# First unit's inverse from diagonal blocks of 16 with one more merge level, its norms from squares by feature, and a new order of steps

## The chip, the cores and the metric

The kernel runs on one core of a Trainium2 chip. The metric is the device time of one execution in microseconds. A profile of one execution gives each instruction's engine, start and length: PE is the matrix engine (PEld its weight loads), DVE the vector engine, ACT the scalar engine, POOL the GpSimd engine, SP the queue that issues the DMAs.

## What is computed

Two layers. The first is a delta-rule recurrence over 768 tokens for 4 batches and 8 heads of width 48; the second is a mixture of four causal attention experts, of which two per token are kept.

```python
k_n = k / (norm(k) + 1e-6)
for t in range(S):                          # state: 48 x 48 per batch and head
    y[t] = q[t] @ state
    state = state + beta[t] * outer(k_n[t], v[t] - k_n[t] @ state)
x = y, heads side by side                   # 768 x 384 per batch
logits = x @ w_gate                         # the two largest of four are kept; softmax over them
for e in range(4):
    a = softmax(causal(q_e k_e^T / 8))      # q_e, k_e, v_e = x @ wq[e], wk[e], wv[e], width 64
    out += weight(e) * (a @ v_e) @ wo[e]
```

## The kernel before

The recurrence is done in blocks of 64 tokens. Within a block the 64 updates follow from the inverse of a unit triangular 64 x 64 matrix, made of the Gram matrix of the block's keys, beta and the norms; from block to block only the state is carried. The work is cut into 6 units (half of the batches, a third of the tokens: units 0 to 2 and 3 to 5 are two sequences of three), and each unit has 4 chunks (index c) of one 64-token block for 16 heads.

For unit n the steps are, by their names in the order list:

- lg, lq, lc: loads of keys, queries and the keys with values. `gr` (L211): Gram matrices on PE, copied to the tile tt. `gq` (L229): K times Q, masked by DVE.
- `si` (L238): DVE transposes the 32 x 32 blocks of tt into B, so that one partition holds one matrix of 32 x 32. `pre` 0 to 5 (L258): the norms by three Newton steps from the sums of squares ss, the factors aa (beta over norm squared), and B times -aa.
- `sv` (L308): the inverse, 30 rank-one steps of a multiply (L305) and an add (L303), then two finishing instructions. For units 1 to 5 it runs on POOL. For unit 0 rows 0 to 8 run on DVE, each instruction cut in two halves, and rows 9 to 31 on POOL (`sg`, L325).
- `so`, `sn` (L338, L334): DVE transposes the inverse back to tt and, untransposed, to TN. `m10` to `m15` (merge1, L343) and `m2n.c` (merge2, L353): matmuls that join the two 32-blocks of each 64-block.
- `ks`, `u`, `q`, `s`, `y` per chunk: the chain proper. u needs the merged inverse, s makes the next state. `hx` spreads the result by DMA.
- `pj`, `pv`: projections; `mx`, `mp`, `mr`, `sc`, `av`, `nm`, `ft`, `fo`: attention and output; `gt`: gates.

The first unit's norms come from a separate load of its keys by token (kt): `sq` (L250) squares on POOL, `sr` (L255) sums on DVE. For units 1 to 5 ss is the diagonal of the Gram matrix.

All instructions of all engines are issued in the order of the list `ORDER` (L35), written out by hand or by a planner: each engine runs its own instructions in that order and waits by semaphores for the others. An entry `+N` is N fillers: matmuls of zeros into a corner of the tile po that nobody reads. The list has 382 of them, one more is issued at the top; 297 stand ahead of u0.0. PSUM tiles named pm_ have three buffers, so a group of matmuls waits until the copies of an earlier group are done. B and tt have two buffers each: unit n + 2 can begin its `gr` when unit n's chain is done with tt. Profile lines with L109 are matmuls, whatever step they belong to.

Of the kernel before, what the change touches and what calls it, by code (L numbers as in the profile page):

```python
# [40 lines left out]
+109 gq0.0 so0 +33 gq0.3 +11 m10.0 w0 sn0 m10.1 +3 m20.0 lg2.0 w5 si1 pre1.0 pre1.1 m20.3 u0.0 pre1.2 pre1.3 w2 m20.2  # L41
s0.0 w1 lc0.2 vt0.2 m20.1 ks0.1 y0.0 pre1.4 gq0.2 u0.1 +3 q0.1 s0.1 vs lq1.3 lq1.2 pre1.5 sv1.1 lc0.3 gq1.0 ks0.2 y0.1
gr2.0 +4 gq1.1 hx0.1.0 sv1.2 q0.2 u0.2 +5 s0.2 lq2.0 gq1.2 vt0.3 sv1.3 +1 ks0.3 gq1.3 y0.2 +1 pj0.0.2 q0.3 lg2.1 u0.3
pj0.0.0 lg2.3 sv1.4 sv1.5 s0.3 sv1.6 y0.3 gr2.3 lg2.2 sv1.7 +6 pv0.0.1 sv1.8 gq2.0 pv0.0.0 sv1.9 sv1.10 sv1.11 sv1.12
sv1.13 mx0.0.0.1 sv1.14 sv1.15 lc1.0 vt1.0 sv1.16 mx0.1.0.0 mx0.0.0.0 lq2.1 w6 mx0.1.0.1 sv1.17 sv1.18 +1 gq2.1 sv1.19
# [745 lines left out]
```

## Time and profile before

| | |
|---|---|
| times of 3 runs | 523.9 us median, 519.34 to 529.47 |
| the profiled execution | 521.83 us, span 520.0 us |
| busy | PE 465.0, PEld 408.9, DVE 320.4, ACT 261.1, POOL 245.9 us |
| fillers | 383, 51.9 us of PE's busy time |
| inputs and outputs | HBM read 24.74 MB, written 4.72 MB |

A row of a timeline is start, length, engine, line, operation, written tile <- read tiles, shapes, count; a bracket at the end is the idle time of the engine before it and what ended it ("issue": nothing that the profile shows). A row of a table of stretches is the stretch, its length, and each engine's busy time in it with the count of instructions. A matmul of fp32 data shows as two passes.

### The profile page before, as it was taken

The page shows a single profiled execution, that of the slowest core. Times are in us where ns is not written, and L with a number is a line of the kernel's source. Part 1 is how long each engine was busy: PE and PEld are TensorE (multiplying, and loading weights), DVE is VectorE, ACT ScalarE, POOL GpSimd, SP SyncE. Part 2 cuts the span into 40 slices and gives each one's busy share as a digit, 9 for nine tenths or more (in the row PEclk, how much of TensorE's full clock was granted, in tenths as well). Part 3 has the DMA queues.
Part 4 walks back from the last instruction along what each step waited for, and adds up shares of the span by engine and source line. Part 5 has one row for each costly group of instructions (what it writes and reads, how often), then busy time and mean ns, then how long its engine had stood idle before and what let it go on. Part 6 is the DMA issues. An engine that isn't in the chain of part 4 may idle for free.

```text
span 520.0 us, 23164 instructions
## 1 busy us (share of the span) xinstructions
PE 465.0 (89%) x10271; PEld 408.9 (79%) x10271; DVE 320.4 (62%) x745; ACT 261.1 (50%) x642; POOL 245.9 (47%) x422
## 2 busy tenths in 40 slices
...
DMA packets 19396, 33.31 MB, mean 64 GB/s; under 512 B 2912, under 2 KB 9440, under 8 KB 19296
## 3 DMA queue, kind: packets, MB, share of 16 engines
...
q14 instruction: 19, 0.16, 0.1%
HBM read 24.74 MB, written 4.72 MB: 57 GB/s over the span
## 4 chain that ended last, share of the span: by engine, by line
PE 68%; DVE 15%; ACT 9%; issue 6%; DMA 1%; SPq 0%; ACTq 0%; DVEq 0%
PE po L109 13%; PE xu L109 7%; PE py L109 6%; DVE tm L305 2%; DVE B L303 2%; ACT QA L486 2%; ACT QA L483 1%; DVE mx L564 1%; ACT KH L489 1%; ACT KA L483 1%; DVE QL L494 1%; DVE KA L492 1%; DVE B L243 1%; DVE B L240 1%; ACT VS L510 1%
## 5 line engine op out<-in xcount | busy, mean ns | idle before, releaser
L303 POOL TENSOR_TENSOR B<-B,tm 128x30 f32<-128x30 f32 (+9 forms) x150 | 78.6, 524 | 11.7
L305 POOL TENSOR_TENSOR tm<-B 128x30 f32<-128x30 f32 (+9 forms) x150 | 74.3, 495 | 10.9
L109 PE MATMUL po<-VS,at 128*64 128x65 f32 x1344 | 51.8, 230 | 6.6 <-ACT rs L634 4.5
L109 PEld LDWEIGHTS po<-VS,at 128*64 128x64 f32 x1344 | 45.0, 142 | 13.0 <-ACT rs L634 5.9
L109 PE MATMUL po<-zb 128*128 128x252 bf16 x383 | 51.9, 287 | 2.5 <-ACT rs L634 1.3
L141 POOL TENSOR_TENSOR kv<-kv,nt 128x384 f32<-128x384 f32 x24 | 19.9, 830 | 60.9 <-DMA kv<-in_kv_dram 48.6
L109 PEld LDWEIGHTS <-zb 128*128 128x128 bf16 x383 | 37.7, 103 | 8.8 <-DVE zb L114 1.1
L372 POOL MEMSET tt<- 32x1024 f32 x10 | 9.5, 946 | 49.6 <-PE pm__2366 L109 13.0
L633 ACT ACTIVATE os<-po 128x128 f32<-128x128 f32 x48 | 13.3, 278 | 35.1 <-PE po L109 35.0
L109 PE MATMUL py<-qf,sb 48*48 48x64 f32 x704 | 24.5, 218 | 2.3 <-issue 1.9
L446 ACT ACTIVATE xh<-py 112x384 fp32r<-112x384 f32 x24 | 11.8, 492 | 28.4 <-PE py L109 28.4
L448 DVE TENSOR_TENSOR xh<-py,xh 112x384 fp32r<-112x384 f32 x24 | 13.4, 557 | 20.4 <-ACT h L447 20.4
L109 PEld LDWEIGHTS <-identb 128*128 128x128 bf16 x192 | 19.2, 100 | 8.2 <-issue 2.0
L294 POOL TENSOR_TENSOR B<-B,nn 128x1024 f32<-128x1024 f32 x5 | 11.9, 2371 | 28.5 <-DVE nn L293 28.4
L109 PEld LDWEIGHTS py<-qf,sb 48*48 48x48 f32 x704 | 21.3, 120 | 5.0 <-issue 2.4
L427 DVE TENSOR_TENSOR sb<-sb,xu 112x384 f32<-112x384 f32 x20 | 11.1, 553 | 22.2 <-PE xu L109 22.1
L109 PE MATMUL py<-pm,ub 64*48 64x64 f32 x768 | 18.0, 228 | 5.2 <-issue 5.0
L409 DVE TENSOR_TENSOR xs<-kv,xu 128x384 f32<-128x384 f32 x22 | 12.1, 552 | 14.8 <-PE xu L109 8.1
L243 DVE STREAM_TRANSPOSE B<-tt 32x1024 f32<-32x1024 f32 x10 | 19.9, 1994 | 0.2
L109 PE MATMUL xu<-sb,kf 48*64 48x48 f32 x704 | 16.8, 229 | 3.6 <-issue 3.2
L109 PEld LDWEIGHTS py<-pm,ub 64*48 64x48 f32 x768 | 14.6, 129 | 6.1 <-issue 5.6
L109 PE MATMUL xu<-xs,tt 64*64 64x48 f32 x768 | 18.5, 227 | 0.8 <-issue 0.7
...
## 6 DMA issues: line engine op xcount, KB each, us to landing
...
kf<-in_kq_dram SPq DMA_DIRECT2D x24, 256.0 KB, 4.1
qf<-in_kq_dram SPq DMA_DIRECT2D x24, 256.0 KB, 3.5
...
wst<-in_wqk_dram SPq DMA_DIRECT2D x3, 256.0 KB, 4.8
wst<-in_wvg_dram SPq DMA_DIRECT2D x1, 256.0 KB, 6.2
```

Of the source, the lines that this page charges most:

```text
L109: T.matmul(o, lhsT=a, rhs=b, start=start, stop=stop, skip_group_check=True)
L141: G.tensor_tensor(vt, vt, PR[n]["nt"][:, c * NP:c * NP + NP, None].to_broadcast([128, NP, HD]), op=OP.mult)
L243: V.transpose(B[r:r + 32], gf[r:r + 32, :, 0:32].rearrange("p t j -> p j t"))
L294: G.tensor_tensor(B, B, bc(nn, 32), op=OP.mult)
L303: e.tensor_tensor(X[:, a:b, i + 1:], X[:, a:b, i + 1:], tv, op=OP.add)
L305: e.tensor_tensor(tv, R[:, :, i + 1:].to_broadcast([128, w, m]), X[:, a:b, i:i + 1].to_broadcast([128, w, m]), op=OP.mult)
L409: V.tensor_tensor(eight(XB), eight(vt), PX, op=OP.subtract)
L427: V.tensor_tensor(eight(new), eight(state(n, c)), SP, op=OP.add)
L446: S.activation(hi, Y[:, :, 0:3], AF.Copy)
L448: V.tensor_tensor(lo, Y[:, :, 0:3], hi, op=OP.subtract)
L483: S.activation((KA if isk else qa)[h, es, :, t], P[h], AF.Copy)
L633: S.activation(os[:, :, e], O[:, :, 0:EH], AF.Copy)
```

## The change

Unit 0 no longer inverts 32 x 32 matrices. The Gram mask keeps only the two diagonal 16 x 16 blocks of each, 14 steps on DVE invert both at once (28 instructions of 2 x i x (15 - i) elements a partition), and nothing of it runs on POOL. The off-diagonal block goes, negated, from the Gram's PSUM to a new tile GO by one more ACT copy per half chunk. After so0 and sn0 a new level `m00.c.0`, `m00.c.1` (merge0) joins the 16-blocks: 32 matmuls and an ACT copy, then 64 matmuls and two DVE adds, into tt and TN. merge1 of unit 0 is cut in four parts instead of two.

The norms of unit 0 come from the keys by feature that are loaded anyway: ACT squares the tile (into the other tt buffer), 16 matmuls a chunk with a column of ones sum over the features into the tile xu, and one DVE copy moves the 32 sums to ss. The kt input is gone. Unit 1's keys are now loaded at the top, ahead of the first kv and q. The memsets of QL and KH stand at the top, with ten for the new tiles.

`ORDER` is new throughout. It has 384 fillers, of which 254 stand ahead of u0.0; si1 and the first norm steps of unit 1 stand between sn0 and the new level. Units 1 to 5 have the same steps as before.

```diff
--- before.py
+++ after.py
...
+NL = 1
...
 ORDER = """
-fr3 +41 gr0.3 sq0 sr0 sq1 sr1 sq2 +8 gr0.0 sq3 sr2 sr3 lq1.1 pre0.0 +4 gr0.1 lg1.3 pre0.1 pre0.2 pre0.3 lg1.1 kc3 fr1
-kc1 fr0 +6 gr0.2 pre0.4 vt0.0 cb si0 pre0.5 kc0 sv0.1 sv0.2 sv0.3 sv0.4 sv0.5 sv0.6 sv0.7 fr2 sg10 sv0.8 sv0.9 sg11
-lc0.1 sv0.10 sv0.11 sg12 w3 sv0.12 sv0.13 sv0.14 sv0.15 lg1.0 +31 gr1.1 sg13 sg14 sg15 vt0.1 sv0.16 lq1.0 sv0.17
-sv0.18 lg1.2 sv0.19 ks0.0 sv0.20 sv0.21 +33 gr1.2 sv0.22 sv0.23 sv0.24 sv0.25 +4 gr1.3 sv0.26 sg16 sg17 sg18 sg19 sg20
-sg21 sg22 kc2 sg23 sv0.27 +4 gr1.0 sg24 sg25 sg26 sg27 sg28 +10 gq0.1 sv0.28 sv0.29 sv0.30 sg29 sg30 sv0.32 sg32 w4
...
++39 gr0.2 sq3 sq0 sq2 +12 gr0.1 +5 sr0 lc0.1 sq1 sr2 gr1.2 +3 sr1 +6 gq0.1 sr3 pre0.0 pre0.1 +1 gr1.0 pre0.2 w0 pre0.3
+pre0.4 +4 gr1.1 +5 gr0.3 +13 gr0.0 si0 pre0.5 sv0.1 +7 gr1.3 sv0.2 +4 gq0.3 sv0.3 sv0.4 sv0.5 sv0.6 sv0.7 sv0.8 sv0.9
+sv0.10 sv0.11 sv0.12 sv0.13 +19 gq0.0 lq1.0 +57 gq1.0 sv0.14 sv0.16 so0 w4 sn0 si1 pre1.0 lq1.1 pre1.1 +32 m00.0.0
+m00.1.0 w3 vt0.0 +31 m00.0.1 cb pre1.2 pre1.3 +9 m10.0 kc2 +7 m20.0 pre1.4 m00.1.1 ks0.0 u0.0 +5 s0.0 pre1.5 sv1.1 w2
+sv1.2 vt0.1 m10.1 m00.3.0 kc3 kc1 m20.1 sv1.3 kc0 m00.2.0 ks0.1 +9 m00.2.1 sv1.4 sv1.5 m00.3.1 m10.2 m10.3 y0.0 u0.1
+sv1.6 sv1.7 sv1.8 lg2.1 sv1.9 sv1.10 gq0.2 sv1.11 lc0.2 sv1.12 sv1.13 sv1.14 q0.1 vs1 s0.1 vt0.2 +6 ks0.2 y0.1 m20.2
...
-    KT = [KF[:, 384 * c:384 * c + 384] for c in range(CH)]
+    cst = cp.tile([128, 240], F32, name="cst")
+    bta = cp.tile([128, NU, 32], F32, name="bta")
+    csb = wk.tile([128, 264], F32, name="csb", tag="at", bufs=5)
+    load_k(0, 0)
+    nc.sync.dma_start(cst, consts[:, 0:240])
+    for c in range(1, CH):
+        load_k(0, c)
+    nc.sync.dma_start(bta, beta)
     for c in range(CH):
-        load_k(0, c)
-    cst = cp.tile([128, 240], F32, name="cst")
-    for c in range(CH):
-        nc.sync.dma_start(KT[c], kt[c])
-        if c == 1:
-            nc.sync.dma_start(cst, consts[:, 0:240])
-    bta = cp.tile([128, NU, 32], F32, name="bta")
-    nc.sync.dma_start(bta, beta)
+        load_k(1, c)
     load_chain(0, 0)
-    csb = wk.tile([128, 264], F32, name="csb", tag="at", bufs=5)
     nc.sync.dma_start(csb, consts[:, 240:504])
     for c in range(CH):
         load_q(0, c)
+    on = cp.tile([128, 1], F32, name="on")
+    V.memset(on, 1.0)
...
-    def free_rows(r, e):
-        G.memset(QL[64 - r:128 - r, e].bitcast(F32), 0.0)
-        G.memset(KH[64 - r:128 - r, e].bitcast(F32), 0.0)
+    slot = lambda k, h: KF[:, 260 * k + 256 * h:260 * k + 256 * h + 256].rearrange("p (t i) -> p t i", t=NP)
+    GO = [[slot(k, h) for k in ks for h in range(2)] for ks in ((0, 8), (4, 10))]
+    AS = [slot(2, h) for h in range(2)]
+    for c in range(CH):
+        G.memset(GO[0][c], 0.0)
+    for t in AS + GO[1]:
+        G.memset(t, 0.0)
+    for r, x in HA:
+        G.memset(QL[64 - r:128 - r, x::2].bitcast(F32), 0.0)
+        G.memset(KH[64 - r:128 - r, x::2].bitcast(F32), 0.0)
...
-    NSV = 1
-    PS = 9
-    BP = KF[:, 0:(32 - PS) * 32].rearrange("p (a b) -> p a b", b=32)
-    SQ = [KF[:, 1536 + 384 * c:1920 + 384 * c] for c in range(CH)]
-    WS = [KF[:, 1536:2592].rearrange("p (a b) -> p a b", b=32)] + LB
+    SQ = [TG[1][:, NP * c:NP * c + NP] for c in range(CH)]
...
         for p, i, _, r, t, _ in by(1):
-            if n:
+            if n >= NL:
                 mm(g[i // 4][t:t + 64, i % 4], x[r:r + HD, p], x[r:r + HD, p], True)
                 continue
             for h in range(2):
...
                 V.tensor_tensor(o[:, :, 32:], g[f][:, :, 32:], kmask[:, None, :].to_broadcast([128, 4, 32]), op=OP.mult)
                 S.activation(o[:, :, 0:32], g[f][:, :, 0:32], AF.Copy)
+            if n < NL:
+                S.activation(GO[n][c][:, 4 * f:4 * f + 4, 0:16], g[f][:, :, 32:48], AF.Copy, scale=-1.0)
...
         if c == 0:
             solve_vars(0)
-        G.tensor_tensor(SQ[c], KT[c], KT[c], op=OP.mult)
+        S.activation(SQ[c], LD[0, c], AF.Square)
     def square_sum(c):
-        V.tensor_reduce(PR[0]["ss"][:, NP * c:NP * c + NP], SQ[c].rearrange("p (a b) -> p a b", b=HD), axis=AX.X, op=OP.add)
+        for p, i, _, r, t, _ in by(1):
+            mm(XS[t:t + 64, i // 4, 4 * c + i % 4:4 * c + i % 4 + 1], SQ[c][r:r + HD, p], on[r:r + HD], True)
+        if c == CH - 1:
+            V.tensor_copy(PR[0]["ss"].rearrange("p (c f i) -> p f c i", c=CH, f=2), XS[:, :, 0:16].rearrange("p f (c i) -> p f c i", c=CH))
...
-            B = pr["B"]
-            bc = lambda t, w: t[:, None, :].to_broadcast([128, w, 32])
-            if n < NSV:
-                for a, b in ((PS, 32), (0, PS)):
-                    V.scalar_tensor_tensor(B[:, a:b], B[:, a:b], -1.0, bc(aa, b - a), op0=OP.mult, op1=OP.mult)
-                S.activation(BP, B[:, PS:], AF.Copy)
+            e = G if n else V
+            if n < NL:
+                Z = blocks(n)
+                V.tensor_scalar(nn, aa, -1.0, None, op0=OP.mult)
+                e.tensor_tensor(Z, Z, by_col(nn), op=OP.mult)
             else:
                 V.tensor_scalar(nn, aa, -1.0, None, op0=OP.mult)
-                G.tensor_tensor(B, B, bc(nn, 32), op=OP.mult)
...
+                G.tensor_tensor(pr["B"], pr["B"], nn[:, None, :].to_broadcast([128, 32, 32]), op=OP.mult)
+    def blocks(n):
+        z = LB[n % 2].rearrange("p a b -> p (a b)").rearrange("p (s x) -> p s x", s=2)[:, :, 16:528]
+        return z.rearrange("p s (a c) -> p s a c", c=32)[:, :, :, 16:32]
+    by_col = lambda t: t.rearrange("p (s i) -> p s i", s=2)[:, :, None, :].to_broadcast([128, 2, 16, 16])
+    by_row = lambda t: t.rearrange("p (s j) -> p s j", s=2)[:, :, :, None].to_broadcast([128, 2, 16, 16])
     def solve_step(n, i):
         B, aa = PR[n]["B"], PR[n]["aa"]
-        tmp = TM
-        e = V if n < NSV else G
-        r = PS if n < NSV else 32
-        if i <= 30:
-            w = min(i, r)
-            h = w // 2 if n < NSV else 0
-            rank1(e, B, B[:, i:i + 1], tmp, i, [x for x in ((0, h), (h, w)) if x[0] < x[1]])
-        elif i == 31:
+        e, size = G if n else V, 16 if n < NL else 32
+        Z = blocks(n) if n < NL else B[:, None]
+        k = 2 if n < NL else 1
+        if i < size - 1:
+            m = size - 1 - i
+            tv = TM[:, 0:k * i * m].rearrange("p (s a b) -> p s a b", s=k, a=i)
+            bc = lambda x: x.to_broadcast([128, k, i, m])
+            if k == 1:
+                Z, tv = B, tv[:, 0]
+                bc = lambda x: x.to_broadcast([128, i, m])
+                e.tensor_tensor(tv, bc(Z[:, i:i + 1, i + 1:]), bc(Z[:, 0:i, i:i + 1]), op=OP.mult)
+                e.tensor_tensor(Z[:, 0:i, i + 1:], Z[:, 0:i, i + 1:], tv, op=OP.add)
+            else:
+                e.tensor_tensor(tv, bc(Z[:, :, i:i + 1, i + 1:]), bc(Z[:, :, 0:i, i:i + 1]), op=OP.mult)
+                e.tensor_tensor(Z[:, :, 0:i, i + 1:], Z[:, :, 0:i, i + 1:], tv, op=OP.add)
+        elif i == size - 1:
             if n:
                 G.affine_select(B, B, pattern=[[-1, 32], [1, 32]], compare_op=OP.is_gt, fill=0.0, base=0,
                                 channel_multiplier=0)
+            if 0 < n < NL:
+                G.memset(B[:, 0:16, 16:32], 0.0)
         else:
-            e.tensor_tensor(B[:, 0:r], B[:, 0:r], aa[:, 0:r, None].to_broadcast([128, r, 32]), op=OP.mult)
-            e.tensor_copy(B.rearrange("p j i -> p (j i)")[:, 0:33 * r - 32:33], aa[:, 0:r])
...
+            if n < NL:
+                e.tensor_tensor(Z, Z, by_row(aa), op=OP.mult)
+            else:
+                e.tensor_tensor(B, B, aa[:, :, None].to_broadcast([128, 32, 32]), op=OP.mult)
+            e.tensor_copy(B.rearrange("p j i -> p (j i)")[:, 0:1024:33], aa)
     def st_nat(n):
         pr = PR[n]
...
     def st_out(n):
         V.transpose(TG[n % 2][:, :, 32:].rearrange("p t i -> p i t"), PR[n]["B"].rearrange("p l i -> p i l"))
-    lanes = lambda n: WS[0] if n == 0 else LB[n % 2]
+    def merge0(n, c, k):
+        tt, a, GR = TG[n % 2], AS[c % 2], range(0, 128, 32)
+        W = ps.tile([128, 2, NP, 16], F32, name="pm_", bufs=3)
+        for i in range(NP):
+            t = NP * c + i
+            for g in GR:
+                if k == 0:
+                    mm(W[g:g + 32, 0, i], GO[n][c][g:g + 32, i], tt[g:g + 32, t, 48:64], True)
+                else:
+                    mm(W[g:g + 32, 0, i], TN[g:g + 32, t], a[g:g + 32, i, 16:32], True)
+                    mm(W[g:g + 32, 1, i], a[g:g + 32, i], TN[g:g + 32, t, 0:16], True)
+        if k == 0:
+            S.activation(a[:, :, 16:32], W[:, 0], AF.Copy)
+        else:
+            for j, o in enumerate((tt[:, NP * c:NP * c + NP, 48:64], TN[:, NP * c:NP * c + NP, 0:16])):
+                V.tensor_tensor(o, o, W[:, j], op=OP.add)
+    lanes = lambda n: LB[n % 2]
     def merge1(n, k):
-        gf = TG[n % 2]
-        W = ps.tile([128, 16, 32], F32, name="pm_", bufs=3)
-        for i in range(16):
-            t = 16 * k + i
+        gf, m = TG[n % 2], NP if n < NL else 16
+        W = ps.tile([128, m, 32], F32, name="pm_", bufs=3)
+        for i in range(m):
+            t = m * k + i
             for r, _ in HA:
                 mm(W[r:r + 32, i], gf[r + 32:r + 64, t, 0:32], gf[r + 32:r + 64, t, 32:64], True)
         for r, _ in HA:
-            S.activation(lanes(n)[r:r + 32, 1 + 16 * k:17 + 16 * k], W[r:r + 32], AF.Copy, scale=-1.0)
+            S.activation(lanes(n)[r:r + 32, 1 + m * k:1 + m * k + m], W[r:r + 32], AF.Copy, scale=-1.0)
...
-    step("vs", ones)
-    for i in (*range(PS + 1, 31), 32):
-        step("sg", solve_pool, i)
+    for k in range(3):
+        step("vs", ones, k)
...
+                step("m0", merge0, n, k, j)
...
-    c[:, 208:240] = (i % 32)[:, None] >= np.arange(32)[None, :]
+    c[:, 208:240] = ((i % 32)[:, None] >= np.arange(32)) & ((i % 32 // 16)[:, None] == np.arange(32) // 16)
...
```

More of the change, by code (lines that the diff above doesn't have):

```diff
@@ L41 @@
[L41 to L45, printed above, removed]
@@ new lines @@
++5 u0.2 m20.3 lq1.2 sv1.15 sv1.16 sv1.17 sv1.18 sv1.19 sv1.20 lc0.3 vt0.3 w1 w5 hx0.1.0 q0.2 sv1.21 gq1.1 s0.2 vs0
+sv1.22 +2 pv0.0.0 lq1.3 gr2.1 ks0.3 lc1.0 vt1.0 sv1.23 y0.2 w6 lg2.2 pj0.0.2 sv1.24 sv1.25 gq1.3 q0.3 lq2.1 u0.3 +11
+y0.3 s0.3 pv0.0.1 gr2.2 sv1.26 sv1.27 sv1.28 +4 gq1.2 ks1.0 +1 gq2.1 sv1.29 sv1.30 hx0.3.0 lg3.0 sv1.31 sv1.32 so1
+lg2.3 pj0.0.0 sn1 pj0.1.0 pj0.1.2 q1.0 lq2.0 m11.0 +11 m11.1 cl1 m21.0 mx0.1.1.3 pv0.1.0 mx0.0.1.3 lg2.0 mx0.0.1.2
+lq2.2 u1.0 mx0.0.0.0 vs2 mx0.0.0.1 mx0.1.1.2 mp0.0 mx0.1.0.1 lc1.1 mx0.1.0.0 s1.0 mr0.0 mp0.1 pv0.1.1 m21.1 vt1.1 gt0
@@ new lines @@
+ks1.1 gr2.3 y1.0 sc0.0.0.0 lc1.3 vt1.3 mr0.1 +1 gr2.0 si2 u1.1 q1.1 lq2.3 sc0.0.3.0 lg3.1 sc0.0.2.0 pre2.0 sc0.0.1.0
+av0.0.0 m21.3 av0.0.3 s1.1 sc0.1.2.0 av0.0.1 m21.2 av0.0.2 lc1.2 pre2.1 pre2.2 vt1.2 gq2.2 ks1.2 y1.1 sc0.1.1.0
+sc0.1.0.0 sc0.1.3.0 u1.2 nm0.0 lg3.2 pre2.3 q1.2 pre2.4 gr3.2 pre2.5 ft0.0 av0.1.3 hx1.1.0 s1.2 sv2.1 gq2.3 sv2.2
+sv2.3 sv2.4 sv2.5 +3 ks1.3 lg3.3 sv2.6 y1.2 gq2.0 sv2.7 lq3.0 pj1.0.2 sv2.8 sv2.9 pj1.0.0 q1.3 u1.3 lq3.1 fo0.0.0
+mx1.0.0.1 sv2.10 sv2.11 av0.1.0 sv2.12 sv2.13 s1.3 sv2.14 sv2.15 sv2.16 lc2.0 y1.3 gr3.3 sv2.17 mx1.1.0.0 sv2.18 +1
@@ L96, with tile_kernel @@
+mx5.1.0.0 sc5.0.3.2 mx5.1.0.6 mp5.1 sc5.0.3.0 ft4.1 pv5.1.1 mr5.1 av5.0.3 sc5.1.0.0 sc5.1.0.1 sc5.1.0.2 sc5.1.1.2
+sc5.1.1.0 av5.1.0 sc5.1.1.1 sc5.1.2.2 sc5.1.2.1 av5.1.1 sc5.1.2.0 fo4.1.1 sc5.1.3.0 gt5 sc5.1.3.1 nm5.0 av5.1.2
+sc5.1.3.2 fo4.1.0 ft5.0 av5.1.3 fo5.0.1 fo5.0.0 nm5.1 ft5.1 +13 fo5.1.1 fo5.1.0
 """
 @with_exitstack
-def tile_kernel(ctx, tc, kq, kv, kt, beta, wqk, wvg, wo, consts, out):
+def tile_kernel(ctx, tc, kq, kv, beta, wqk, wvg, wo, consts, out):
     nc = tc.nc
@@ L240, in st_in @@
         V.transpose(B, gf[:, :, 32:].rearrange("p t j -> p j t"))
-        if n:
+        if n >= NL:
             for r, _ in HA:
```

124 lines of the change are left out of this document (47 added, 77 removed).

## The prediction

> **What bounds the kernel now.** I read the page first: the span, the busy shares, the groups, the chain that ended last.
>
> ```profile
> span 520.0 us, 23164 instructions
> PE 465.0 (89%) x10271; PEld 408.9 (79%) x10271; DVE 320.4 (62%) x745; ACT 261.1 (50%) x642; POOL 245.9 (47%) x422
> PE 68%; DVE 15%; ACT 9%; issue 6%; DMA 1%; SPq 0%; ACTq 0%; DVEq 0%
> L109 PE MATMUL po<-zb 128*128 128x252 bf16 x383 | 51.9, 287 | 2.5 <-ACT rs L634 1.3
> ```
>
> PE is busy for 465.0 of 520.0 us, and 51.9 us of that are 383 fillers, which compute nothing. Next I asked for each engine's busy time by stretches; the columns are PE, PEld, DVE, ACT and POOL busy (with counts), granted clock, DMA share, GB/s.
>
> ```profile
> 0.00:20.00 20.00, 16.56 (x347) 12.80 (x347) 10.64 (x30) 8.30 (x20) 11.53 (x17) 0.91 0.89 312
> 20.00:49.00 29.00, 25.48 (x371) 21.61 (x371) 28.69 (x126) 8.40 (x17) 19.91 (x47) 0.94 0.07 18
> 49.00:58.10 9.10, 8.69 (x323) 7.34 (x321) 9.05 (x10) 4.06 (x7) 1.27 (x1) 1.00 0.20 73
> 58.10:76.00 17.90, 12.47 (x591) 10.81 (x590) 12.36 (x32) 6.12 (x15) 9.27 (x12) 1.00 0.27 80
> 127.00:520.00 393.00, 356.93 (x7816) 317.69 (x7816) 225.16 (x487) 211.21 (x521) 169.60 (x284) 0.98 0.18 54
> ```
>
> From 20 to 49 us DVE is never free (28.69 of 29.00): the first unit's 32-step inverse. From 127 us to the end PE is busy 91% of the time: there it is PE's queue that sets the end, and a gain ahead of it counts only as far as PE's own sum falls. How the start hangs together, in the timelines of DVE, ACT and POOL (start, length):
>
> ```profile
> 14.11 0.34 DVE L269 RECIPROCAL rr<-g 128x32 f32<-128x32 f32 x1
> 17.97 0.19 DVE L284 TENSOR_TENSOR aa<-nn,bta 128x32 f32<-128x32 f32 x1
> 18.08 1.97 DVE L240 STREAM_TRANSPOSE B<-tt 128x1024 f32<-128x1024 f32 x1
> 21.41 0.19 DVE L305 TENSOR_TENSOR tm<-B 128x30 f32<-128x30 f32 x1
> 21.63 0.19 DVE L303 TENSOR_TENSOR B<-B,tm 128x30 f32<-128x30 f32 x1
> 49.59 1.96 DVE L339 STREAM_TRANSPOSE tt<-B 128x1024 f32<-128x1024 f32 x1
> 51.48 0.42 DVE L236 TENSOR_TENSOR pm<-pm__928,cst 128x256 f32<-128x256 f32 x1
> 52.16 1.94 DVE L336 STREAM_TRANSPOSE tn<-B 128x1024 f32<-128x1024 f32 x1
> 55.87 3.92 DVE L243 STREAM_TRANSPOSE B<-tt 32x1024 f32<-32x1024 f32 x2
> 65.05 0.56 DVE L409 TENSOR_TENSOR xs<-kv,xu 128x384 f32<-128x384 f32 x1 [0.39 <-PE xu L109]
> 57.02 0.60 ACT L365 ACTIVATE tt<-pm__1037 128x512 f32<-128x512 f32 x1
> 70.21 2.35 POOL L294 TENSOR_TENSOR B<-B,nn 128x1024 f32<-128x1024 f32 x1 [3.57 <-DVE nn L293]
> ```
>
> Norms and transpose until 20 us, steps until 49, the transposes so0 and sn0 until 54.1, two merge levels, and then (the chain, below) u0.0 at 58.13. Unit 1's solve begins on POOL at 70.21 + 2.35 = 72.6.
>
> **The change, part by part.** PE's prices come from three stretches that hold one kind of work each, and from the fillers of the start:
>
> ```profile
> 7.03:7.82 0.79, 0.79 (x65) 1.00 1.08 394
> 20.00:20.62 0.62, 0.62 (x33) 1.00 0.26 85
> 52.66:54.80 2.14, 2.14 (x129) 1.00 0.03 8
> 0.00:58.10 58.10, 37.64 (x298) 0.00 (x0) 0.00 (x0) 0.94 0.37 128
> 1.13 5.97 PE po L109 x42
> 58.13 0.61 PE xu L109 x32
> ```
>
> The first is one gr0 of 64 passes (each fp32 matmul shows as two): 12.3 ns a pass. The second is one gr1 of 32, 0.62 us; I price a gq alike. The third is m10.0 and m10.1, 128 passes, 16.7 ns each. The fourth is the fillers alone: 0.126 us each up to 58.1; the other 85 take (51.9 - 37.64)/85 = 0.168.
>
> *Norms.* The kt loads, POOL's squares and DVE's four reductions go; four Square activations and 64 one-column matmuls (128 passes, 1.6 us at the gram's rate) come. In PE's order sr3 stands behind 65 fillers (8.2 us), two gr0 (1.6), a gr1 and a gq (1.2) and the other sr: 1.1 + 8.2 + 2.8 + 1.6 = 13.7 us. The Newton steps then take what they take now, 14.11 to 18.16, so aa is there at about 18.5. But gr0.0, the last gram, stands behind 88 fillers (11.1), three gr0 and itself (3.2), three gr1 (1.9), a gq (0.6) and the sr (1.6): 19.5 us. So si0 starts at 20.2, against 18.08. Now it costs 2.1 us.
>
> *Steps.* 28 instructions instead of the 30 steps in halves. The 30-element ones follow each other every 0.22 us; 112 elements, the largest, cost 0.31 by the 384-element row (0.56). At their mean of 80 elements I take 0.27, so 7.5 us. With the transpose (2.0), the sign and beta multiply (0.95, 512 elements scaled from 384), three gq masks (0.68 each by L236, 2.1) and the last multiply with its copy (1.0), DVE reaches so0 at 20.2 + 13.5 = 33.7. sv0.14 is queued behind gq1.0's mask, which PE gives only after 87 more fillers (11.0), gr1.3 and three gq (2.5): 33.0, then mask and last step: so0 at 35.2, 14.4 us earlier than 49.59; sn0 ends at 39.1 instead of 54.1. POOL no longer takes part; nobody waits for that.
>
> *New level.* m00 is 4 chunks x (64 + 128) passes = 768; at 12.3 ns 9.4 us. No row has matmuls of 16 columns. Ends: 3.1 ns, if time goes with columns from the 64-column gram, and 16.7 of m10; with sr 2.8 to 15.0 us, and I take the gram's 11.0, whose weights are also 32 columns wide. [...]
>
> m00.0.1 ends in two DVE adds, and in DVE's queue these stand behind si1 (1.97 + 3.92), pre1.0 and pre1.1 (1.6): 39.1 + 7.5 + 0.6 = 47.2. PE has its own part done by 44.3 (32 fillers, two first halves, 31 fillers, the second half). Then m10.0 (0.5), ACT's copy (0.6), m20.0 (1.1), m00.1.1 (1.6): u0.0 at 51.1 without a stall like this one at the start, 53.4 with it. I take 52.3, 5.8 before 58.13. Who waits for the adds is PE, with m10.0 and all behind it. pre1.5 follows s0.0, so unit 1's solve begins at about 57, 15 us earlier.
>
> ```profile
> PE pm__279 L109 <- issue: 2.3, 1, 2.3
> PE pm__874 L109 <- DVE pm L236: 3.5, 1, 3.5
> PE py L109 <- issue: 6.9, 7, 1.4
> PE xu L109 <- issue: 4.5, 7, 1.1
> 0.00:58.10 58.10, 50.73 (x1038) 41.75 (x1038) 48.38 (x163) 20.77 (x43) 32.71 (x65) 0.94 0.37 128
> 58.10:520.00 461.90, 414.32 (x9239) 367.14 (x9237) 272.04 (x583) 240.33 (x600) 213.18 (x357) 0.97 0.19 56
> ```
>
> *What PE still has to do then.* Before: 414.3 us of work and 47.6 us of waits. Now also: chunks 2 and 3 of m00 (4.7), m10.1 to m10.3 (1.6), one m20 more (1.1), less gq1.0, which has moved ahead (0.6), and 130 fillers instead of 85 (45 x 0.168 = 7.6): 14.3. All four chunks' merges stand between u0.0 and u0.1 in the new order. The fillers cost nothing where PE would wait anyway (the 109 ahead of gq0.0 were followed by 3.5 us more of waiting) and all of it where not; I take half, 3.8.
>
> *The rest.* POOL is busy for 11.5 of its first 20 us, with squares and memsets; the squares go, and of the new memsets the four that gr0's copies wait for come first, under the first 39 fillers of PE. Without that cover gr0.2's copies would wait for them, a memset each. Unit 1's keys are now loaded ahead of kv and q, on SP's queue past both; their first user, gq0.1, is 12 us in, and a late load there would hold sr3 behind it. w0 moves from behind m10.0 to the Newton steps: its load goes out on SP behind lc0.1, and its copy stands in ACT's queue ahead of the copies of gr1.1, gr0.3 and gr0.0; I cost it at nothing, since some 5 us of PE's work lie between, and (c) holds the other case. Units 1 to 5 compute what they did; the new order only moves their steps.
>
> *Sum.* 52.3 + 414.3 + (14.3 - 3.8) + 47.6 = 524.7 us of span; with the 1.8 us outside the span (521.83 - 520.0) 526.5. The start gains 5.8, PE's queue takes 10.5 back. The runs shown have their median at 523.9, 2.1 above the profiled one; all is reckoned from 521.83. The bounds: m00 and sr -3.5 or +1.7 (what of them is not covered by waits), fillers 3.8 either way, the stall 1.2: 518 to 533.
>
> **Rivals.** (a) *Faster: the solves, not PE, pace the units.* If what comes behind waits for each unit's inverse, all moves up by the 15 us that so0 and unit 1's solve gain: 507. For it: DVE holds 15% of the chain. Against: PE is 91% busy after 127 us, fillers number 384 instead of 382, so the waits that they stand for have not gone, and 507 would need 524.7 - 505 = 20 us off the 47.6.
>
> (b) *Slower: many tiny matmuls starve PE.* From 58.1 to 76 us, where small matmuls are densest, PE stands still for 5.4 of 17.9 us with 591 passes, mostly with no releaser named ("issue"). The 896 new passes, at 5.4/591, would add 8.2 us, and their price at m10's 16.7 ns 4.0 more: 539. It decides if these gaps come with the number of instructions. Against: fillers around m00 are long and give PE's queue time. [...] No row here says what the gaps are.
>
> (c) *The start does not get shorter.*
>
> ```profile
> wst<-in_wqk_dram SPq DMA_DIRECT2D x3, 256.0 KB, 4.8
> ```
>
> If ACT stands at w0's copy for such a load (4.8 us from issue to landing), the gram copies behind it keep their PSUM buffers, gr0.0 waits for one, and with it si0 and all to u0.0; with a stall like today's beside it u0.0 is at 58.1 again: 526.5 + 5.8 = 532.
>
> **How the numbers follow.** Two per cent, about what a measurement here can tell, is 10.4 us: below 511.4 is faster, above 532.2 slower. Forecast 0.50 (slower 0.05 of it, else within), (a) 0.20 (faster 0.15, the rest falls short), (b) 0.22 (slower 0.20), (c) 0.08 (slower 0.04). So faster 0.15, same 0.56, slower 0.29. The forecast's own range is 518 to 533; 510 to 540 leaves out most of (a)'s lower half and (b)'s upper end, about 0.2.
>
> **What would show it.** so0 near 35 and u0.0 near 52 us show the start; PE's busy time near 476 us (465 + 11) with waits near 50 shows the sum. Wrong: m00's passes far from 12 ns; waits below 40 us (then a) or above 60 (then b); u0.0 after 57 (then c).

## The result and the profile after

Four executions of the changed kernel have their median at 502.1 us (500.28 to 505.31), four of the kernel before, beside them, at 525.1 (519.34 to 529.47). The ratio is 0.960 (95% interval 0.950 to 0.971): faster by 4%, where 526.5 us and no change were forecast. Medians, here and below, are over all executions; ratios leave out those that ran in a slower state of the chip. The page of the changed kernel's profiled execution (500.28 us), with the rows that answer to those of before:

```profile
span 498.6 us, 24842 instructions
PE 468.2 (94%) x11169; PEld 415.2 (83%) x11169; DVE 298.0 (60%) x661; ACT 264.0 (53%) x659; POOL 228.5 (46%) x382
PEclk9699975999999999999999999999999999999999
PE 77%; DVE 10%; issue 5%; ACT 3%; SPq 3%; DMA 2%; ACTq 0%; DVEq 0%
L109 PE MATMUL po<-zb 128*128 128x252 bf16 x385 | 53.3, 288 | 3.0 <-issue 1.4
```

PE holds 77% of the chain instead of 68, and its idle time has fallen from 55.0 to 30.4 us (span less busy). The timelines of DVE and POOL show the start:

```profile
42.73 1.96 DVE L346 STREAM_TRANSPOSE tt<-B 128x1024 f32<-128x1024 f32 x1
60.91 0.29 DVE L364 TENSOR_TENSOR tt<-tt,pm__1090 128x128 f32<-128x128 f32 x1 [4.24 <-PE pm__1090 L109]
61.57 2.35 POOL L301 TENSOR_TENSOR B<-B,nn 128x1024 f32<-128x1024 f32 x1 [12.34 <-DVE nn L300]
```

Busy times and counts of its engines up to u0.0 and behind it (columns as in the prediction):

```profile
0.00:60.86 60.86, 52.60 (x1379) 42.82 (x1382) 34.17 (x92) 16.62 (x48) 13.94 (x22) 0.92 0.28 97
60.86:498.60 437.74, 415.59 (x9794) 372.41 (x9794) 263.87 (x569) 247.40 (x611) 214.56 (x360) 0.98 0.20 61
```

So0 is at 42.73 (before 49.59, forecast 35.2), and u0.0 at 60.86 (before 58.13, forecast 52.3): the start did not get shorter but 2.7 us longer. Behind u0.0 PE works 415.6 us, about what it did before (414.3), and waits 437.74 - 415.59 = 22.2 us, where it waited 47.6. The gain is there. The waits of PE behind 127 us, the longest rows of each kernel (total, times, longest), first before, then after:

```profile
PE py L109 <- issue: 4.9, 5, 1.4
PE po L109 <- ACT rs L634: 4.0, 9, 0.5
PE pm__4732 L109 <- DVE ol L654: 2.8, 1, 2.8
PE po L109 <- issue: 2.1, 1, 2.1
PE xu L109 <- issue: 2.0, 4, 1.0
PE pm__6693 L109 <- issue: 1.6, 1, 1.6
PE pm__4329 L109 <- DVE QL L494: 1.6, 1, 1.6
```

```profile
PE pm__5035 L109 <- DVE KA L517: 1.2, 1, 1.2
PE pm__4442 L109 <- DVE pm L241: 1.1, 1, 1.1
PE xu L109 <- issue: 0.9, 2, 0.6
PE pm__4942 L109 <- DVE ol L679: 0.7, 1, 0.7
```

All rows of that view sum to 32.0 us before (11.5 without a releaser, 20.5 with one) and to 8.5 after (1.7 and 6.8). No single wait is large; most of the many small ones are gone, of both kinds.

### The profile page after: what moved, and what is told of

The parts are those of the page before. It is cut to its first block, busy times and chain, and to the rows that moved or that the text cites. A ratio compares the mean times of both kernels' runs of the same rounds, so it can differ in the third digit from the quotient of the medians.

```text
span 498.6 us, 24842 instructions
## 1 busy us (share of the span) xinstructions
PE 468.2 (94%) x11169; PEld 415.2 (83%) x11169; DVE 298.0 (60%) x661; ACT 264.0 (53%) x659; POOL 228.5 (46%) x382
## 4 chain that ended last, share of the span: by engine, by line
PE 77%; DVE 10%; issue 5%; ACT 3%; SPq 3%; DMA 2%; ACTq 0%; DVEq 0%
PE po L109 15%; PE xu L109 7%; PE py L109 6%; SPq L480 2%; DVE mx L589 1%; DVE tt L346 1%; DMA xh<-h 1%; DVE tn L343 1%; DVE B L248 1%; DVE B L245 1%; DMA kf<-in_kq_dram 1%; DVE KA L517 1%; DVE QL L519 1%; ACT QA L511 0%; PE pm__3152 L109 0%
## 5 line engine op out<-in xcount | busy, mean ns | idle before, releaser
L324 POOL TENSOR_TENSOR B<-B,tm 128x30 f32<-128x30 f32 (+9 forms) x150 | 79.6, 530 | 11.8
L109 PE MATMUL po<-zb 128*128 128x252 bf16 x385 | 53.3, 288 | 3.0 <-issue 1.4
L109 PE MATMUL po<-VS,at 128*64 128x65 f32 x1344 | 49.8, 226 | 0.1
L109 PEld LDWEIGHTS po<-VS,at 128*64 128x64 f32 x1344 | 43.1, 138 | 5.8 <-issue 1.9
L658 ACT ACTIVATE os<-po 128x128 f32<-128x128 f32 x48 | 13.3, 278 | 26.8 <-PE po L109 26.5
L440 ACT ACTIVATE ub<-xu 128x384 f32<-128x384 f32 x24 | 11.8, 490 | 13.6 <-PE xu L109 11.2
L109 PEld LDWEIGHTS xu<-xs,tt 64*64 64x64 f32 x768 | 14.6, 138 | 3.8 <-issue 1.7
L109 PE MATMUL py<-pm,ub 64*48 64x64 f32 x768 | 16.0, 221 | 0.6 <-issue 0.6
```

What stands on the lines that cost most here:

```text
L109: T.matmul(o, lhsT=a, rhs=b, start=start, stop=stop, skip_group_check=True)
L324: e.tensor_tensor(Z[:, 0:i, i + 1:], Z[:, 0:i, i + 1:], tv, op=OP.add)
L440: S.activation(eight(UB), PX, AF.Copy)
L658: S.activation(os[:, :, e], O[:, :, 0:EH], AF.Copy)
```

## The experiments

Theory A: the gain is the new order of the later steps; the new inverse is worth nothing or costs. Theory B: it is the shorter start, which what follows is tied to.

**The two orders cut at u0.1.** One kernel computes as the changed one and takes the new order up to u0.1 and the old one behind; the other is the kernel before with the old order up to u0.1 and the new one behind. In each, whatever either order has done by the cut stands ahead of it, so that the second has gq1.0, pre1.5 and five solve steps of unit 1 ahead of u0.1. The first lines of its edit:

```diff
-s0.0 w1 lc0.2 vt0.2 m20.1 ks0.1 y0.0 pre1.4 gq0.2 u0.1 +3 q0.1 s0.1 vs lq1.3 lq1.2 pre1.5 sv1.1 lc0.3 gq1.0 ks0.2 y0.1
...
+s0.0 w1 lc0.2 vt0.2 m20.1 ks0.1 y0.0 pre1.4 gq0.2 gq1.0 pre1.5 sv1.1 sv1.2 sv1.3 sv1.4 sv1.5 u0.1 sv1.6 sv1.7 sv1.8
+lg2.1 sv1.9 sv1.10 sv1.11 sv1.12 sv1.13 sv1.14 q0.1 vs s0.1 +6 ks0.2 y0.1 +5 u0.2 lq1.2 sv1.15 sv1.16 sv1.17 sv1.18
...
```

> The changed kernel with its own steps and order up to u0.1, and from there the order of before for all that is left. In the profiles u0.1's result is copied at 82.6 us after the change and at 66.5 before it. Theory A (the gain is the order of the later steps, and the new start loses time): u0.1 at about 82, then the 453.5 us that before needs from there, so a span of 530 to 536, slower than before by 2 to 3%. Theory B (the new start with its earlier first solve is what lets the later steps run closer): near the changed kernel, 498 to 508.

> The kernel before with its own steps and order up to u0.1, and from there the new order for all that is left (unit 0 inverted in blocks of 32, norms from the keys by token). Theory A: u0.1 at about 66 and then at best the 416 us that the changed kernel needs from there, 482; unit 1's solve ends no earlier than in the changed kernel (about 115 us), so 485 to 502, as fast as the changed kernel or faster. Theory B: near before, 515 to 525.

New start with old rest: 537.8 us, ratio 1.033 (1.024 to 1.042), span 533.9. Old start with new rest: 502.2 us, 0.963 (0.956 to 0.971), span 502.7, with the old inverse, the old norms and no m00. A holds (530 to 536, and 485 to 502, which the second misses by 0.7 us), B does not: as far as these runs can tell, the order of the later steps is the whole gain. With it behind, the old start and the new one end alike (502.2 and 502.1 us); with the old order behind, the new start costs 3%, the cut itself included.

**The later steps alone, from u1.0.** The kernel before, old order up to u1.0, new from there.

```diff
 ... av0.0.0 m11.0 m11.1 cl1 +6 m21.0 nm0.0 pre2.5 sc0.1.3.0 +5
-u1.0 lq2.2 m21.2 sv2.1 s1.0 m21.1 ks1.1 y1.0 ft0.0 u1.1
+lq2.2 u1.0 s1.0 m21.1 ks1.1 y1.0 lc1.3 vt1.3 +1 u1.1
```

> The kernel before, computing as it did, in its old order of steps up to u1.0 (133 us), and from there in the new order. With the old order up to u0.1 the new rest gave 0.963 and a span of 502.7. If the gain lies in the order of the later steps (u1.0 to the end: unnamed waits and the waits for QL, KA, rs, ol behind 127 us, 32.0 us against 8.5), most of it stays: span 502 to 508. If it lies in what the new order does between u0.1 and u1.0 (so1 at 112.7 instead of 121.6), most of it goes: span 512 to 518.

Measured 501.3 us, 0.971 (0.963 to 0.979), beside a kernel before at 518.3 us: some 15 us. The span is 498.4 us. The two profiled executions differ by more, 520.0 - 498.4 = 21.6 us, so what follows overstates the gain by some of the difference between executions. Busy times from u1.0 to the end, and the fillers there, of the kernel before and of this one:

```profile
133.50:520.00 386.50, 350.43 (x7595) 311.97 (x7591) 221.77 (x471) 206.75 (x511) 165.93 (x282) 0.98 0.18 55
L109 PE MATMUL po<-zb 128*128 128x252 bf16 x31 | 5.0, 272 | 0.9 <-ACT rs L634 0.9
```

```profile
132.90:498.40 365.50, 347.67 (x7640) 310.55 (x7640) 222.93 (x471) 206.75 (x511) 167.69 (x282) 0.99 0.19 58
L110 PE MATMUL po<-zb 128*128 128x252 bf16 x76 | 11.1, 272 | 0.4 <-ACT rs L635 0.4
```

Both reach u1.0 at 133 us; then the same work takes 21.0 us less. Idle time goes from 36.1 to 17.8 us; of the single waits over 0.15 us, those without a releaser go from 11.5 to 2.7 us in sum and those with one from 20.5 to 11.3. Busy time goes down by 2.8 although 45 more fillers add 6.1: the useful work shows 8.9 us less. Part of that is the clock, 0.98 against 0.99 in the mean: 17.8 us at half clock behind u1.0 in the kernel before and 8.1 in this one, by the clock's record. Half of the difference, 4.9 us, is my estimate of the most that this is worth; the rest I did not separate. Some waits in the old order are followed by such stretches, as here in the kernel before, behind the wait of 2.8 us for ol (granted clock 0.54 in the mean of these 7 us):

```profile
267.00:274.00 7.00, 7.00 (x69) 6.67 (x68) 4.10 (x17) 2.30 (x6) 0.00 (x0) 0.54 0.00 0
```

**Cut at u3.0.** New order from u1.0 to u3.0 with the old one behind, and old order to u3.0 with the new one behind, both in the kernel before and, as above, with whatever either order has done by the cut ahead of it. From the edit of the second:

```diff
 ... sc2.0.3.0 mx2.1.1.10 cl3
-u3.0 mx2.1.1.11 mx2.1.1.12 s3.0 mx2.1.1.13 m23.1 sv4.3 sv4.4
+gq3.3 lq4.2 gq4.0 lg5.0 fo1.1.0 u3.0 vt3.1 s3.0 lc3.2 m23.1 ks3.1 y3.0
```

> The kernel before in its old order up to u1.0, the new order from there to u3.0, and the old order again behind. The old order to u1.0 with all the new rest had a span of 498.4 us, 365.5 of them behind u1.0 against 386.5 in the kernel before; in that kernel the way from u1.0 to u3.0 took 151.9 us before and 131.5 then, and from u3.0 to the end 234.6 and 234.0. If the gain lies between u1.0 and u3.0: span 498 to 503. If it only moved across u3.0 (more done ahead of it, less behind) and both parts hold some of it: span 506 to 514. If it lies behind u3.0: 516 to 522.

> The kernel before in its old order up to u3.0 (285 us) and in the new order from there on; the opposite cut gave 1.011 of the time before. If the gain lies in the order behind u3.0: span 500 to 507. If each part alone gives nothing, because the old order has done unit 2's scores by u3.0 and the new one only then does them: 515 to 521.

523.3 us, 1.011 (1.004 to 1.018); and 519.9 us, 0.993 (0.988 to 0.998). The first span, 519.5 us, pointed to the order behind u3.0, and the second, 520.8, refutes that. Neither part gives more than a trace of the gain, though both together give all of it. My argument for it is that the new order starts unit 3's chain (u3.0 at 265.4 us instead of 285.4) with unit 2's wide score and maximum steps still to do, and has them to lay between the small steps behind; a cut at u3.0 spends them first. The orders bear out the first half of it: behind u3.0 stand 24 sc and 23 mx steps of unit 2 in the new one, 12 and 6 in the old. The second cut agrees in its time; that this is the reason was not shown, since the profiled executions of both cuts had other clocks (0.85 throughout, and a stretch of 17 us at half) and their waits cannot be set beside the others'.

**Do the solves pace the units?** Rival (a) of the prediction. First unit 1's solve started earlier in the changed kernel; then 22 of the 30 POOL steps of the solves of units 3 and 5 left out of both kernels, so that these inverses are incomplete.

```diff
-m20.0 pre1.4 m00.1.1 ks0.0 u0.0 +5 s0.0 pre1.5 sv1.1 w2
+m20.0 pre1.4 pre1.5 sv1.1 sv1.2 sv1.3 sv1.4 sv1.5 m00.1.1 ks0.0 u0.0 +5 s0.0 w2
```

> The changed kernel with unit 1's last scaling (pre1.5) and its first five solve steps moved ahead of m00.1.1, whose two additions DVE waited 4.2 us for, and seven later solve steps moved ahead of the POOL operations that waited for ACT (w1, w5) and for a buffer (vt1.0). Nothing of PE's work changes. Theory S (POOL's solve of unit 1 sets when everything behind it can start): POOL's first product at 57 instead of 61.6 us, so1 at 107 to 109 instead of 113.5, and the end as much earlier: span 493 to 496. Rival P (PE's sum of work and instruction supply sets the end, so1 only looks like it): so1 earlier, span 497 to 500.

```diff
-sv3.8 sv3.9 sv3.10
+sv3.8
```

> The kernel before without 22 of the 30 solve steps of units 3 and 5 on POOL (some 33 us of each solve; those two inverses are left incomplete). So3 at 275.3 and so5 at 412.4 us, with 107.6 us from so5 to the end in both kernels. If the solves pace the units (rival (a) of the prediction): the span falls by 15 us or more, to 505 or less. If PE's queue paces them and the solves lie beside it: the solve of unit 5 ends near 370, but u5.0 and the end move by 5 us at most: 515 to 520.

> The same steps left out of the changed kernel. If the solves pace it: span 470 to 485. If PE's queue does, and its fillers ahead of so3 and so5 are all that stands there for the solves: 494 to 499.

```profile
56.95 2.35 POOL L301 TENSOR_TENSOR B<-B,nn 128x1024 f32<-128x1024 f32 x1 [7.94 <-DVE nn L300]
```

In the first, POOL starts at 56.95 instead of 61.57 us and has unit 1's inverse ready at 108.5 instead of 113.4 us, and the time is 502.2 us as without it. This says little about unit 1, since the gain stayed on POOL: so1 came at 111.37 instead of 113.46 us and sn1 at 116.81, as before it (116.83), each at its place in DVE's queue.

The short solves say more. Unit 5's solve ends on POOL with a copy at 403.05 us in the kernel before and at 369.17 with the steps left out, but so5, the transpose that hands it on, moves by only 7.4 us. First the two rows of the kernel before, in which the solve is done 9 us ahead of so5 already, then those of the run:

```profile
403.05 0.24 POOL L323 COPY B<-aa 128x32 f32<-128x32 f32 x1
412.39 2.03 DVE L339 STREAM_TRANSPOSE tt<-B 128x1024 f32<-128x1024 f32 x1
```

```profile
369.17 0.24 POOL L321 COPY B<-aa 128x32 f32<-128x32 f32 x1
404.96 2.01 DVE L337 STREAM_TRANSPOSE tt<-B 128x1024 f32<-128x1024 f32 x1
```

The kernel before takes 516.8 us so (0.992, 0.986 to 0.997; span 513.3, a little below the 515 that I wrote down) and the changed one 499.6 (0.961, where it has 0.960 with whole solves; span 496.9). POOL is busy for 48 us less in each (197.5 instead of 245.9 us in the kernel before), and that buys some 4 us in the kernel before and nothing that these runs can tell in the changed one. PE's queue paces the kernel, and the solves of units 3 and 5 lie beside it; those of units 2 and 4 I did not try. The 385 us between so1 and the end in two kernels, on which my theory S for these runs rested, are no rule: with the early solve they were 501.2 - 111.37 = 389.8.

**Where the unnamed waits stand.** I counted the instructions of PE's queue in the trace: weight loads, matmuls and semaphore instructions, in order. Each unnamed wait over 0.25 us, 20 of 20 before and 14 of 14 after, stands at instruction 192 or 193 of a block of 256. Five of the changed kernel's:

```
start us  wait   instruction  modulo 256
 53.10    0.81     2240          192
 60.55    2.12     2752          192
 64.28    0.86     3008          192
 67.83    1.85     3265          193
 76.11    2.60     3777          193
```

The named waits stand anywhere. The page's row of the queue q8, before and after, counts as many packets as PE's queue has such blocks: 81, and 7 more with the 896 passes (1792 instructions) of m00 and sr:

```profile
q8 instruction: 81, 1.33, 1.1%
```

```profile
q8 instruction: 88, 1.44, 1.2%
```

Counted in the same way, 16 of the 61 blocks behind 127 us held less than 3.6 us of PE's work in the kernel before, and 4 of 61 in the changed one. A short block by itself need not take as long: the shortest of the kernel before took 2.54 us.

To measure it by itself I put small matmuls behind the last output of the changed kernel.

```diff
+    def tiny(k):
+        g = 32 * (k % 4)
+        mm(PO[g:g + 32, 260:276], ident[g:g + 32, 0:32], ident[g:g + 32, 0:16], False)
+
+    for k in range(640):
+        tiny(k)
+    for _ in range(320):
+        filler()
+    for k in range(320):
+        tiny(k)
+        filler()
```

> The changed kernel with three stretches behind its last output, on PE alone, with no wait in them: 640 fp32 matmuls of 32 x 32 with 16 columns (1280 passes, ten blocks of 256 instructions); 320 fillers; 320 times one such matmul and one filler (960 passes, 7.5 blocks). Rival T (instruction supply): the first stretch takes 33 to 42 us, that is 26 to 33 ns a pass, with an unnamed wait every 128 passes and 10 to 13 ns a pass between them; the fillers take 40 us (0.126 each) without such waits; the mixed stretch 47 to 50 us, the small ones adding only 20 to 30 ns each, without waits. If small passes simply run at the rate that I priced (12.3 ns): the first stretch takes 13 to 16 us, with no waits. [...]

PE's timeline in the three stretches:

```profile
494.85 2.04 PE L109 MATMUL po<-cst 32*32 32x16 f32 x223
499.57 1.90 PE L109 MATMUL po<-cst 32*32 32x16 f32 x128 [2.68 <-issue]
503.04 1.90 PE L109 MATMUL po<-cst 32*32 32x16 f32 x128 [1.57 <-issue]
506.51 1.90 PE L109 MATMUL po<-cst 32*32 32x16 f32 x128 [1.57 <-issue]
...
528.16 0.63 PE L109 MATMUL po<-cst 32*32 32x16 f32 x33 [1.84 <-issue]
528.72 36.87 PE L109 MATMUL po<-zb 128*128 128x252 bf16 x320
565.52 0.23 PE L109 MATMUL po<-cst 32*32 32x16 f32 x2
565.68 0.28 PE L109 MATMUL po<-zb 128*128 128x252 bf16 x1
565.89 0.23 PE L109 MATMUL po<-cst 32*32 32x16 f32 x2
566.05 0.28 PE L109 MATMUL po<-zb 128*128 128x252 bf16 x1
...
586.29 0.29 PE L109 MATMUL po<-cst 32*32 32x16 f32 x2
586.51 0.39 PE L109 MATMUL po<-zb 128*128 128x252 bf16 x1
586.83 0.29 PE L109 MATMUL po<-cst 32*32 32x16 f32 x2
```

Busy times from the first of these waits to the last, and in the mixed stretch from 600 us on:

```profile
499.57:528.16 28.59, 15.20 (x1024) 14.38 (x1024) 0.00 (x0) 0.00 (x0) 0.00 (x0) 0.50 0.02 5
600.00:736.00 136.00, 135.94 (x756) 70.79 (x754) 0.00 (x0) 0.00 (x0) 0.00 (x0) 0.50 0.00 1
```

The queue q8 in the first window (packets, MB, share of the DMA engines):

```profile
q8 instruction: 8, 0.13, 1.8%
```

The first row is the time before the first wait: 223 passes take 2.04 us, 9.1 ns each. Then PE does 128 passes and waits, eight times over: eight blocks, eight packets of 16 KB, 28.59 / 8 = 3.57 us a block, 27.9 ns a pass. The granted clock is 0.50 there, and passes take 14.8 ns; at full clock two blocks in the start of the changed kernel, from 60.55 to 67.83 us in the table above, took 3.73 and 3.55 us. With the fillers between there is no such wait: PE is busy for 135.94 of 136.00 us. What T forecast of the waits in the first stretch holds: one every 128 passes, eight of eight, with one packet of q8 to a block. That PE waits there for its next instructions is my reading; no row names what it waits for.

I missed on the mixed stretch: not 0.15 but 0.37 us a pair (565.68 to 566.05), and 0.54 (586.29 to 586.83) after the clock had fallen to half at 571 us (granted 1.00 from 535 to 560 us, 0.78 from 560 to 580, 0.50 behind). A filler alone took 36.87 / 320 = 0.115 us. So at full clock one small matmul beside one filler cost some 0.26 us, though the two passes take 0.02 to 0.06 us in the first stretch. What this is I did not separate.

**What the joining level costs.** The changed kernel without the m00 steps: unit 0's blocks of 16 stay unjoined.

```diff
-+32 m00.0.0 m00.1.0 w3 vt0.0 +31 m00.0.1 cb pre1.2 pre1.3
++32 w3 vt0.0 +31 cb pre1.2 pre1.3
```

> The changed kernel without the steps m00 (the two 16-blocks are not joined, so unit 0's inverse is incomplete; everything else is done). The price of the new level. 768 passes at about 11 ns are 8.5 us of PE; the unnamed waits between 47 and 80 us, next to the m00 groups, are some 10 us more. If both are theirs and PE's queue sets the end: 480 to 485. If only the work is theirs: 489 to 492. If the level is hidden: 497 to 500.

495.2 us, 0.952 (0.946 to 0.957); span 493.6, between the ranges that I wrote down. The unnamed waits from 60 to 127 us go from 11.4 to 0 and u0.1 comes 14 us earlier, but a wait for DVE's xs takes 9.6 us there, and the end gains 5.0 in the span, some 4 us by the ratios.

**The norms and the fillers.** The fillers ahead of gr0.0 from 88 to 41; the old norms in the changed kernel; and the last without the 76 fillers behind u1.0.

```diff
-+39 gr0.2 sq3 sq0 sq2 +12 gr0.1 +5 sr0
++19 gr0.2 sq3 sq0 sq2 +6 gr0.1 +2 sr0
...
```

> The changed kernel with 41 instead of 88 fillers ahead of gr0.0. If PE's queue of fillers sets when unit 0's last gram and its inverse start: si0 comes 6 to 9 us earlier than 28.4 (47 fillers of 0.14 to 0.2 us) and the end moves by nearly as much, 490 to 493. If norms or loads set it, or a colder PE clock takes it back: si0 at 24 or later and 496 to 503.

```diff
-        S.activation(SQ[c], LD[0, c], AF.Square)
+        G.tensor_tensor(SQ[c], SQ[c], SQ[c], op=OP.mult)
...
+        V.tensor_reduce(PR[0]["ss"][:, NP * c:NP * c + NP], SQ[c].rearrange("p (a b) -> p a b", b=HD), axis=AX.X, op=OP.add)
```

> The changed kernel with the first unit's norms as they were: token-major k loaded, squared on POOL, summed on DVE; the 64 one-column matmuls (128 passes) and the four Square activations go. Theory S (what stands ahead of the solve of unit 1 sets the time: in the changed kernel so1 at 113.5 us and the span 385 us later, and 385 us from so1 to the end in the kernel without the joining level as well): the norms are ready before the last gram, si0 near 21 us instead of 28.4, so0 near 37, u0.0 near 54, so1 3 to 6 us earlier, span 492 to 496. Rival T (PE's instruction stream: every one of the unnamed waits of PE falls at instruction 192 or 193 of a block of 256, and where small matmuls are dense a block lasts 3.4 to 4.5 us whatever is in it): from 48 to 96 us the blocks stay back to back, so that what is gained at si0 shrinks to the one block that the norms had (3.7 us) or less: span 495 to 499, and the unnamed waits between 45 and 96 us stay near 12 us.

> The changed kernel with the old norms (span 495.6) without the 76 fillers behind u1.0, 11 us of PE's time. If they are work like any other there: span 485 to 489. If they stand where PE would wait anyway: PE's waits behind 127 us grow from 8 us by as much, span 494 to 497. If waits without fillers also cost the clock (half of it for 3.4 us or more): over 497.

Half the fillers: 502.2 us, si0 at 27.4 instead of 28.4, where 6 to 9 us earlier was the forecast; PE stood for keys (1.6 us) and in an unnamed wait (1.1 us) instead. The old norms: 499.1 us (0.964, 0.958 to 0.970), si0 at 26.8, u0.0 at 59, not 54, since the last sum stands behind gq0.1's mask in DVE's queue, which waits until 18.15 us. The span, 495.6 us, lies in the ranges of both theories and decides nothing between them. Without the late fillers: 499.6 us (0.966, 0.957 to 0.974), span 500.6. Their 11 us do not come back: PE's waits behind 127 us rise from 8.1 to 13.8, and its busy time there falls by only 1.0 us (356.3 to 355.3), with some 10 us more at half clock. The fillers stand where PE would wait; that such waits cost it the clock was not shown, as over the whole span the granted clock was 0.966 without these fillers and 0.965 with them.

**Two small ones.** The pairs of av steps parted in the old order, and a late product moved up in the kernel with the old start and the new rest.

```diff
-av0.1.2 av0.0.2 si2 sc0.0.1.0
+av0.1.2 si2 sc0.0.1.0 av0.0.2
```

> The kernel before with eight of the eleven pairs of av steps that follow each other in PE's queue parted by moving the second behind PE's next step. One named wait of the old order alone: PE for ACT's rs (5.8 us in all, 4.0 behind 127 us). If such waits add up to the end one by one, as PE is never far from busy there: rs waits under 2 us and span 4 to 5 us shorter, 515 to 517. If another wait takes each one's place: span 519 to 521.

```diff
-ks0.2 y0.1 +5 u0.2 lq1.2 sv1.15 sv1.16 sv1.17 sv1.18 sv1.19 sv1.20 lc0.3 vt0.3
+ks0.2 y0.1 lc0.3 +5 u0.2 lq1.2 sv1.15 sv1.16 vt0.3 sv1.17 sv1.18 sv1.19 sv1.20
```

> The old start with the new rest (span 502.7) with one thing mended: the load lc0.3 and POOL's product vt0.3 go earlier, since DVE there waited 14.5 us for that product, and PE 8.3 us behind it, with the clock at half for 10.2 us. If PE's queue sets the end from the start of unit 0's chain on, so that idle time anywhere behind it counts: u0.3 at 88 to 93 us instead of 101.7, span 492 to 497. If only what lies behind u1.0 counts: 499 to 503.

The first: 523.2 us beside 522.2 of the kernel before, 1.012 (1.000 to 1.024). The waits for rs behind 127 us fall from 4.0 to 1.3 us in its trace, whose span of 513.9 us lies below both ranges, yet over the executions the time does not fall: one kind of wait alone is within what these runs can't tell. The second: 507.7 us, 0.977 (0.966 to 0.988), no better than the kernel that it was to mend; u0.3 came at 96.1 us, not at 88 to 93, and waits for QL (5.5 us) took the place. No kernel that computes the whole was clearly below the changed one.

## Why the prediction was wrong

The sum was 52.3 + 414.3 + (14.3 - 3.8) + 47.6 = 524.7 us of span. Measured, by the two windows above: 60.86 + 415.6 + 22.2 = 498.6. (The parts of the 14.3 add up to 14.4; that changes nothing.)

**The waits: -25.4 us, the step that failed.** The prediction carried the 47.6 us of waits over whole and said that "the new order only moves their steps". Cut at u1.0, the order alone took 18.2 us of idle time from the kernel before, between the two profiled executions. I had no row for what the order does and put it at nothing; I should have bounded it from both sides, by nothing and by the 32.0 us that the waits behind 127 us sum to. The orders themselves can be read for it: in the old one eleven pairs of av steps follow each other in PE's queue with at most a filler between, in the new one none. I also took 384 fillers instead of 382 to mean that the waits were still there; but 31 stood behind u1.0 before and 76 do now, so where PE would wait had moved. Against rival (a) I wrote that 507 "would need 524.7 - 505 = 20 us off the 47.6" and took that for unlikely. It is what happened, by another cause. Waits below 40 us, which I had named as the sign of (a), are a sign of more than (a).

**PE's work: -9.2.** 415.6 us instead of 424.8. Busy time was not a fixed sum here: the useful work behind u1.0 showed 8.9 us less in the new order alone, with fewer stretches at half clock.

**The start: +8.6.** Si0 came at 28.36, not 20.2. The sr passes met an unnamed wait of 1.91 us, and from 15 to 25 us the granted clock was 0.50, when six fillers took 1.37 us (16.24 to 17.61) instead of 0.76. So PE was late with both of its parts: the last sums came at 20.06 us, where 13.7 was forecast, and gr0.0, whose end was forecast at 19.5, held DVE until 27.84 us, just ahead of si0:

```profile
13.65 0.56 PE L109 MATMUL xu<-on,tt 48*64 48x1 f32 x25 [1.91 <-issue]
16.24 1.44 PE L109 MATMUL po<-zb 128*128 128x252 bf16 x6
20.06 0.19 DVE L264 COPY ss<-xu 128x32 f32<-128x32 f32 x1 [0.23 <-PE xu L109]
27.84 0.29 DVE L229 TENSOR_TENSOR tt<-pm__532,cst 128x128 f32<-128x128 f32 x1 [1.79 <-PE pm__532 L109]
28.36 1.98 DVE L245 STREAM_TRANSPOSE B<-tt 128x1024 f32<-128x1024 f32 x1
```

The steps on DVE cost what was priced (14.4 us from si0 to so0, forecast 15.0), and from so0 to u0.0 it took 18.1 us against 17.1. POOL's start came late (61.57, forecast 57), as pre1.5 stood behind m00.1.1's additions, 4.24 us. With the early solve POOL started 4.6 us sooner and the end came no earlier.

**m00's price.** The passes alone ran at 10.5 ns each where no unnamed wait stood among them, and some 128 of them took 3.55 us with the wait of 2.12 us at 60.55; the rows are these two stretches of m00:

```profile
44.84:46.19 1.35, 1.35 (x129) 1.32 (x130) 1.35 (x1) 0.28 (x1) 0.00 (x0) 1.00 0.00 0
57.31:60.86 3.55, 1.43 (x132) 1.33 (x126) 0.00 (x0) 1.36 (x3) 0.00 (x0) 1.00 0.02 5
```

So 12.3 ns was fair for a pass, and wrong for 768 of them in one place: from 44.84 to 95.99 us thirteen blocks follow each other at 3.9 us.

**The rivals.** (b) was right in what decides it: the gaps come with the number of instructions (34 of 34 at one place of each 256; 1.57 us and more at each of the burst's blocks), and the changed kernel has ten of them over 0.25 us from 48 to 96 us. It had the wrong place for the end: behind 127 us the new order has fewer blocks of small steps only (4 short blocks instead of 16), and the same gaps nearly vanish (11.5 to 1.7 us). The waits with a releaser fell by more, from 20.5 to 6.8 us; that a new order lowers them is shown by the cut at u1.0, by which steps it does so is not. (c)'s 58.1 us for u0.0 was near, but not by w0's copy. (a)'s mechanism is refuted by the short solves, for units 3 and 5.
